# Causal attention and a cosine MLP on one core: score blocks regrouped in PSUM banks, with another order of masks, exponentials and copies

## The chip, the cores and the metric

The kernel runs on one core of a Trainium2 chip. Its time is the device time of one execution in microseconds (us); the lower the better. The kernel before takes 648.55 us, the median of two runs (647.44 and 649.65).

The core has five engines that run their own instruction streams and wait for each other through semaphores: TensorE (PE in the rows; PEld is its weight load), VectorE (DVE), ScalarE (ACT), GpSimd (POOL) and SyncE (SP), which here only starts transfers. TensorE writes its results to PSUM, here one tile `banks` of eight banks with 512 fp32 values per partition, from which VectorE and ScalarE read.

## The reference

4 batches, 12 heads, 448 tokens, head size 64; then 1792 tokens of width 768 through a two-layer MLP of width 2048 with the activation h cos(h), all in fp32.

```python
scores = scale * np.matmul(q, k.transpose(0, 1, 3, 2))
scores = np.where(mask, -1000000000.0, scores)      # causal
scores = scores - np.max(scores, axis=-1, keepdims=True)
attn = np.exp(scores)
attn = attn / (np.sum(attn, axis=-1, keepdims=True) + 1e-09)
attn_out = np.matmul(attn, v)
...
h = x @ w_in
g = h * np.cos(h)
return g @ w_out
```

## The kernel before

**Attention** is a software pipeline over N = 24 pairs of heads (4 batches, 6 pairs each). One turn `i` of the loop in `attention` works on three pairs at once: the scores and softmax of pair `i` (`cur`), the transposition of the probabilities of pair `i - 1` (`prev`), and the product with v of pair `i - 2` (`old`); it also brings q and k of pair `i + 1` (`nxt`) into place. There is no scheduler: each engine does its instructions in the order in which the code writes them, and a pair's blocks are handed over by semaphores.

The 448 tokens are cut into 7 blocks of 64 rows; R is 64, and block `m` (1 to 7) has `m` x 64 columns, since the rest is masked. Both heads of a pair stand in the two halves of the 128 partitions.

- `transpose_in(i, which, b)` (L310) turns q (`which` 0) or k (1) of a pair by four transpositions of 112 tokens into bank `b`; token 4r + c lies at place c of row r in the loaded tile, so that the transposed tokens come out with c outermost. `evac_in` copies the bank on ScalarE to the tile `flat` (L318) and puts them in order by a write with a step of 4 elements (16 bytes). q goes through bank 2, k through bank 7.
- `scores(i)` (L352) computes the 7 blocks in 8 parts (block 7 in two), 16 matmuls of a 64x64 quarter of the array, in the order 7, 5, 7, 4, 6, 3, 2, 1. Blocks whose `SWAP` is 0 (7, 6, 1) and those with 1 (5, 4, 3, 2) use different quarters, so that one of each kind runs at a time: two lanes. `BANK` says where a block lies: 7 and 1 in bank 4, 6 in 5, 5 and 3 in 6, 4 and 2 in 7. `start` and `stop` are set for the first and the last part in a bank.
- `masked` (L361, VectorE) adds the mask, scales, takes the row's minimum, and writes the tile `pb` in SBUF; `exps` (L369, ScalarE) takes the exponential with that minimum as bias and sums it up; `inverse` (L376, L377, VectorE) makes reciprocals of a group of sums; `normalise` (L383, GpSimd) multiplies. The groups are `HIGH` = 7, 6, 5, at the end of a turn, and `LOW` = 4, 3, 2, 1, at the start of the next. The columns of the small tile `stat` go by block number.
- `tp(i, n, b)` (L401) transposes pieces of `pb` in four groups (4, 2, 4 and 4 of them) with `evac_tp` as copy to the tile `pm`: group 0 through bank 3 (copied by VectorE, L316), group 3 through bank 4 (VectorE), group 2 through bank 5 (ScalarE, L318), group 1 through bank 3 again (ScalarE).
- `av` (L427, L437) multiplies with v into banks 0 and 1; `finish_hi` (L453, ScalarE) writes the rounded high part of the result, `finish_lo` (L457, VectorE) the rest, both to `xa` and `xb`, the input of the MLP.
- Between two turns the main loop adds a piece of weight conversion: two VectorE instructions a turn (L139 and L142 in one, L148 and L152 in the next), and one or two on GpSimd (L145; L156, L157), which stand behind the first group of `normalise`.

In the last turns `fill` adds matmuls of the MLP's first layer (L541 to L543). **The MLP** follows (`moe`, L637 and later lines); in it TensorE works through without a pause, and the change does not touch it.

Of the kernel before, what the change touches and what calls it, by code (L numbers as in the profile page):

```python
# [16 lines left out]
ALU = mybir.AluOpType  # L17
# [4 lines left out]
def kernel(  # L22
# [205 lines left out]
    def attention(filler_of, postponed):  # L228
        with (
# [77 lines left out]
            def transpose_in(i, which, b):  # L307
                t = qkt[i, which] = flat[:, 2 * which + i % 2, 0:S], banks8[:, b, 0:S]
                for c in range(4):
                    nc.tensor.transpose(  # L310
                        t[1][:, c * Q4 : (c + 1) * Q4], nat[i][which][:, c], ident[0:Q4, 0:Q4]
                    )
# [45 lines left out]
            def masked(i, *ms):  # L358
                for m in ms:
# [3 lines left out]
                        scalar=3.0e38, op0=ALU.add, op1=ALU.min, accum_out=stats[i][:, 0, m - 1 : m],  # L363
                    )

            def exps(i, *ms):
                for m in ms:
                    st = stats[i]
                    nc.scalar.activation(  # L369
                        probs(i, m), probs(i, m), AF.Exp, scale=-1.0, bias=st[:, 0, m - 1 : m],  # L370
                        accum_out=st[:, 1, m - 1 : m],
                    )

            def inverse(i, ms):
                st, cs = stats[i], slice(min(ms) - 1, max(ms))
# [3 lines left out]
            def normalise(i, *ms):  # L379
                for m in ms:  # L380
                    p = probs(i, m)
                    r = stats[i][:, 2, m - 1 : m]
# [86 lines left out]
            evac_in(0, 1, True, slice(0, 2))  # L469
            evac_in(0, 1, False, slice(2, 4))  # L470
            transpose_in(0, 0, QB)
            evac_in(0, 0, True, slice(0, 2))
            evac_in(0, 0, False, slice(2, 4))
            keep_warm(7)
            for i in range(N + 4):
# [25 lines left out]
                if cur:  # L501
# [879 lines left out]
```

## Time and profile before

| | |
|---|---|
| median of the runs | 648.55 us (647.44 and 649.65) |
| profiled execution, its own time | 651.7 us |
| its span in the profile | 649.7 us |
| busy: TensorE, VectorE, ScalarE, GpSimd | 611.2, 478.2, 426.4, 454.2 us |
| mean granted clock of TensorE | 0.991 of full speed |

The profile shows one execution; times count from the span's start. A row of the timeline is one instruction, or several alike merged, with its start, its length, engine, line, and in brackets how long the engine was idle ahead of it and whom it waited for. `x4` means four instructions. A matmul's length holds its way through the array, so that rows overlap. The MLP's lines cost the most time in sum; the attention loop stands in the first third of the span.

### The profile page before, as it was taken

What the parts mean: (1) busy time and instruction counts of PE and PEld (TensorE: products, weight loads), DVE (VectorE), ACT (ScalarE), POOL (GpSimd) and SP (SyncE); (2) the same over time, 40 slices, a digit from 0 to 9 for tenths busy, and PEclk for the clock granted to TensorE, in tenths of its full rate; (3) what the DMA queues carried; (4) which work ended last, traced back from release to release, by engine and by line L of the source; (5) the groups of instructions that cost most, each with busy time, mean ns of one, the idle gap of its engine ahead of it and who ended that gap; (6) DMA issues with size and microseconds to landing.
All of it is one profiled execution on the core that took longest, in us unless ns stands there. A gap on an engine that the chain in (4) does not pass through costs nothing.

```text
span 649.7 us, 13426 instructions
## 1 busy us (share of the span) xinstructions
PE 611.2 (94%) x4761; PEld 551.5 (85%) x4761; DVE 478.2 (74%) x1016; ACT 426.4 (66%) x929; POOL 454.2 (70%) x529
## 2 busy tenths in 40 slices
PE   6888888888899999999999999999998999999996
PEld 5666666666678999999999999999998999999996
DVE  3588788888773867887777777774347878887886
ACT  3788788888886677877787777752335446544640
POOL 1566666666672597878787877782566888788894
PEclk9799999999999999999999999999998999999999
DMA  7434655544550586879787878859998485558305
GB/s 158 106 93 114 162 126 127 150 116 117 136 162 9 175 301 253 295 283 307 250 294 259 281 278 258 300 201 355 388 338 299 157 292 201 183 201 291 98 2 145
DMA packets 127234, 134.17 MB, mean 207 GB/s; under 512 B 75296, under 2 KB 111504, under 8 KB 127168
## 3 DMA queue, kind: packets, MB, share of 16 engines
q1 hardware_dynamic: 119424, 106.92, 52.8%
q0 software_dynamic: 4928, 24.78, 10.4%
q10 hardware_dynamic: 2816, 1.64, 0.9%
q8 instruction: 37, 0.61, 0.4%
q14 instruction: 29, 0.24, 0.1%
HBM read 83.36 MB, written 49.94 MB: 205 GB/s over the span
## 4 chain that ended last, share of the span: by engine, by line
PE 86%; DVE 6%; ACT 4%; DMA 2%; issue 1%; ACTq 0%; DVEq 0%
PE banks L637 21%; PE banks L1086 11%; PE banks L1066 11%; PE banks L352 7%; PE banks L542 7%; PE banks L541 7%; PE banks L543 7%; PE banks L437 5%; PE banks L310 3%; ACT flat L318 2%; DVE pm L316 2%; PE banks L1103 2%; PE banks L990 2%; PE banks L401 2%; DVE pb L361 2%; ACT pb L369 1%
## 5 line engine op out<-in xcount | busy, mean ns | idle before, releaser
L383 POOL TENSOR_TENSOR pb<-pb,stat 128x448 f32<-128x448 f32 (+6 forms) x168 | 100.5, 627 | 75.0 <-DVE stat L377 68.5
L625 DVE TENSOR_TENSOR acc<-acc,banks 128x768 f32<-128x768 f32 (+1 forms) x122 | 112.7, 932 | 42.8 <-PE banks L637 32.6
L637 PE MATMUL banks<-w,gh 128*128 128x384 f32 x512 | 109.9, 336 | 0.0
L369 ACT ACTIVATE pb<-pb,stat 128x448 f32<-128x448 f32 (+6 forms) x168 | 85.1, 510 | 34.5 <-DVE stat L361 21.7
L637 PEld LDWEIGHTS banks<-w,gh 128*128 128x128 f32 x512 | 90.8, 188 | 1.6 <-DVE acc L623 0.2
L361 DVE CUSTOM_DVE_ANT_0 pb<-banks,mask 128x448 f32<-128x448 f32 (+6 forms) x168 | 60.9, 417 | 30.4 <-PE banks L352 30.4
L541 PE MATMUL banks<-xa,w 128*128 128x512 f32 x192 | 74.9, 390 | 0.4 <-DVE stat L361 0.4
L542 PE MATMUL banks<-xa,w 128*128 128x512 f32 x192 | 75.3, 392 | 0.0
L543 PE MATMUL banks<-xa,w 128*128 128x512 f32 x192 | 75.1, 391 | 0.0
L401 PE MATMUL banks<-ident,pb 128*128 128x128 f32 x336 | 50.6, 281 | 16.0 <-DVE pm L316 15.9
L637 PE MATMUL banks<-w,gl 128*128 128x384 f32 x256 | 65.2, 335 | 0.0
L661 POOL TENSOR_TENSOR w<-ct,w 128x768 fp32r<-128x768 f32 x28 | 51.9, 1852 | 14.7 <-ACT w L660 12.3
L401 PEld LDWEIGHTS banks<-ident,pb 128*128 128x128 f32 x336 | 38.2, 143 | 21.8 <-DVE pm L316 21.2
L352 PE MATMUL banks<-flat 64*64 64x64 f32 (+5 forms) x768 | 49.5, 380 | 7.1 <-DVE pm L316 2.8
L549 ACT ACTIVATE ni<-banks 128x512 int32<-128x512 f32 (+1 forms) x64 | 34.4, 538 | 32.3 <-PE banks L543 18.6
L352 PEld LDWEIGHTS banks<-flat 64*64 64x64 f32 x768 | 33.6, 141 | 25.2 <-ACT flat L318 10.9
L568 POOL TENSOR_TENSOR gl<-r,gh 128x512 fp32r<-128x512 f32 x32 | 41.5, 1299 | 19.3 <-ACT gh L567 19.1
L551 DVE SCALAR_TENSOR_TENSOR r<-ni,banks 128x512 f32<-128x512 int32 (+1 forms) x56 | 35.1, 626 | 21.7 <-ACT ni L549 21.1
L318 ACT COPY flat<-banks 128x448 f32<-128x448 f32 (+1 forms) x48 | 45.8, 953 | 4.0 <-DVE flat L316 4.0
L553 ACT ACTIVATE r<-r 128x512 f32<-128x512 f32 (+1 forms) x56 | 32.8, 586 | 22.5 <-DVE r L551 22.0
L637 PEld LDWEIGHTS banks<-w,gl 128*128 128x128 f32 x256 | 46.4, 188 | 0.0
L1066 PE MATMUL banks<-xb,bb 128*128 128x384 f32 x234 | 45.4, 338 | 0.0
(138 smaller groups left out, 1511.6 us busy)
## 6 DMA issues: line engine op xcount, KB each, us to landing
bb<-w_in_d SPq DMA_DIRECT2D x48, 384.0 KB, 5.2
land<-in_moe_w_in_dram SPq DMA_DIRECT2D x14, 768.0 KB, 5.5
land<-in_moe_w_out_dram SPq DMA_DIRECT2D x14, 768.0 KB, 5.7
w_out_d<-w POOLq DMA_DIRECT2D x14, 768.0 KB, 5.8
big<-w_out_d SPq DMA_DIRECT2D x25, 384.0 KB, 4.7
land<-in_q_dram SPq DMA_DIRECT2D x48, 112.0 KB, 3.3
w_in_d<-w POOLq DMA_DIRECT2D x7, 768.0 KB, 3.9
raw_d<-ct POOLq DMA_DIRECT2D x14, 384.0 KB, 7.8
```

What stands on the lines that cost most here:

```text
L352: nc.tensor.matmul(place(m)[heads(j ^ SWAP[m]), c : c + z - a], lhsT=qt[heads(j), (m - 1) * R : m * R], rhs=kt[heads(j), a:z], start=banks ...
L361: nc.vector.tensor_tensor_reduce(out=probs(i, m), in0=place(m), in1=mask[:, z : z + m * R], scale=-scale, scalar=3.0e38, op0=ALU.add, op1= ...
L369: nc.scalar.activation(probs(i, m), probs(i, m), AF.Exp, scale=-1.0, bias=st[:, 0, m - 1 : m], accum_out=st[:, 1, m - 1 : m],)
L383: nc.gpsimd.tensor_tensor(p, p, r.to_broadcast(list(p.shape)), op=ALU.mult)
L401: nc.tensor.transpose(banks8[:, b, o + x * P : o + (x + 1) * P], prob[i][:, a * R : (a + 2) * R], ident,)
L541: yield nc.tensor.matmul(hv, lhsT=wh[:, f], rhs=x[:, 0, cc, t], start=(cc == 0), stop=False)
L542: yield nc.tensor.matmul(hv, lhsT=wh[:, f], rhs=x[:, 1, cc, t], start=False, stop=False)
L543: yield nc.tensor.matmul(hv, lhsT=wl[:, f], rhs=x[:, 0, cc, t], start=False, stop=(cc == NCC - 1))
L625: nc.vector.tensor_tensor(d, d, o, op=ALU.subtract)
L637: nc.tensor.matmul(o[:, e, 0:EH], lhsT=a[:, cs], rhs=w[:, e * EH : (e + 1) * EH], start=(x == 0), stop=(x == 5),)
L1066: nc.tensor.matmul(o, lhsT=w[:, u, k * P : (k + 1) * P], rhs=x[k][:, v], start=k + m == 0, stop=k == K - 1 and m == 2,)
L1086: nc.tensor.matmul(o[:, b % 2, 0:EH], lhsT=g_ops[i][u][:, c * P : (c + 1) * P], rhs=wouts[g, i][:, v], start=(x == 0), stop=(x == 2),)
```

## The change

- `BANK`, `parts`: block 7 is alone in bank 4; 6 and 1 share bank 5, 5 and 2 bank 6, 4 and 3 bank 7. The parts come in the order 7, 4, 7, 3, 5, 6, 2, 1.
- Masks come in the order 7, 4, 3, 6, 1, 5, 2 (7, 6, 1, 5, 4, 2, 3 before), exponentials in the order 7, 4, 3, 6, 1, 5, 2 (7, 6, 5, 4, 1, 3, 2 before). The groups for reciprocals and normalisation are `FIRST` = 7, 4, 3 and `SECOND` = 6, 1, 5, 2, and the columns of `stat` go by that order. The reciprocals of `FIRST` follow the masks at once; `finish_hi` stands behind four exponentials (behind two before), and `finish_lo` directly behind it in the code.
- k is transposed through bank 6; group 3 of the probabilities goes through bank 5, group 2 through bank 2.
- q's copy reads the bank with a step and writes straight on; k's four transpositions write the bank with a step of 4 elements, and its copy has no step on either side. The two copies of the first pair, which VectorE and ScalarE share, are cut by rows.

The numbers of instructions stay as they are on every engine.

```diff
             def transpose_in(i, which, b):
                 t = qkt[i, which] = flat[:, 2 * which + i % 2, 0:S], banks8[:, b, 0:S]
+                o = t[1].rearrange("p (r c) -> p c r" if which else "p (c r) -> p c r", c=4)
                 for c in range(4):
-                    nc.tensor.transpose(
-                        t[1][:, c * Q4 : (c + 1) * Q4], nat[i][which][:, c], ident[0:Q4, 0:Q4]
-                    )
+                    nc.tensor.transpose(o[:, c], nat[i][which][:, c], ident[0:Q4, 0:Q4])
...
-            def evac_in(i, which, dve=False, cs=slice(0, 4)):
+            def evac_in(i, which, dve=False, rs=slice(0, Q4)):
                 d, s = qkt[i, which]
-                evac(
-                    d.rearrange("p (r c) -> p c r", c=4)[:, cs],
-                    s.rearrange("p (c r) -> p c r", c=4)[:, cs], dve,
-                )
+                d = d.rearrange("p (r c) -> p r c", c=4)
+                s = s.rearrange("p (r c) -> p r c" if which else "p (c r) -> p r c", c=4)
+                evac(d[:, rs], s[:, rs], dve)
...
-            BANK = {7: (4, 0), 1: (4, 7), 6: (5, 0), 5: (6, 0), 3: (6, 5), 4: (7, 0), 2: (7, 4)}
+            BANK = {7: (4, 0), 6: (5, 0), 1: (5, 6), 5: (6, 0), 2: (6, 5), 4: (7, 0), 3: (7, 4)}
             SWAP = {7: 0, 6: 0, 5: 1, 4: 1, 3: 1, 2: 1, 1: 0}
-            HIGH, LOW = (7, 6, 5), (4, 3, 2, 1)
+            FIRST, SECOND = (7, 4, 3), (6, 1, 5, 2)
+            COL = {m: x for x, m in enumerate(FIRST + SECOND)}
...
                 parts = [
-                    (7, 0, 6 * R, 7 * R), (5, 0, 0, 5 * R), (7, R, 0, 6 * R), (4, 0, 0, 4 * R),
-                    (6, 0, 0, 6 * R), (3, 0, 0, 3 * R), (2, 0, 0, 2 * R), (1, 0, 0, R),
+                    (7, 0, 6 * R, 7 * R), (4, 0, 0, 4 * R), (7, R, 0, 6 * R), (3, 0, 0, 3 * R),
+                    (5, 0, 0, 5 * R), (6, 0, 0, 6 * R), (2, 0, 0, 2 * R), (1, 0, 0, R),
                 ]
...
                 if prev:
-                    inverse(i - 1, LOW)
-                    normalise(i - 1, *LOW)
+                    inverse(i - 1, SECOND)
+                    normalise(i - 1, *SECOND)
                 while postponed:
                     postponed.pop(0)()
                 if cur:
                     exps(i, 7)
+                    masked(i, 4, 3)
+                    exps(i, 4, 3)
                     masked(i, 6, 1)
                     exps(i, 6)
-                    masked(i, 5, 4, 2, 3)
+                    masked(i, 5, 2)
+                    inverse(i, FIRST)
+                    normalise(i, *FIRST)
...
                     av(i - 2)
                     finish_hi(i - 2)
-                if cur:
-                    exps(i, 5)
-                    inverse(i, HIGH)
-                    normalise(i, *HIGH)
-                if old:
                     finish_lo(i - 2)
...
                 if cur:
-                    exps(i, 4)
+                    exps(i, 1)
                 if nxt:
-                    transpose_in(i + 1, 1, 7)
+                    transpose_in(i + 1, 1, 6)
                     evac_in(i + 1, 1)
                 if cur:
-                    exps(i, 1, 3)
+                    exps(i, 5)
                 if prev:
-                    tp(i - 1, 3, 4)
-                    evac_tp(i - 1, 3, 4, True)
-                    tp(i - 1, 2, 5)
-                    evac_tp(i - 1, 2, 5)
+                    tp(i - 1, 3, 5)
+                    evac_tp(i - 1, 3, 5, True)
+                    tp(i - 1, 2, QB)
+                    evac_tp(i - 1, 2, QB)
```

In the instruction streams three places show it. First TensorE, at the end of a turn and the start of the next, before: the last two transpositions (`pb`), then the scores (`flat`), with the engines that an instruction waits for in brackets.

```order
L401 MATMUL banks<-ident,pb_143 128x128 [waits DVE_49]
L401 MATMUL banks<-ident,pb_143 128x128
L352 MATMUL banks<-flat 64x64 [waits DVE_49,Activation_49]
L352 MATMUL banks<-flat 64x64
L352 MATMUL banks<-flat 64x320 x2
L352 MATMUL banks<-flat 64x384 x2
L352 MATMUL banks<-flat 64x256 x2
L352 MATMUL banks<-flat 64x384 [waits Activation_49]
L352 MATMUL banks<-flat 64x384
L352 MATMUL banks<-flat 64x192 x2
L352 MATMUL banks<-flat 64x128 x2
L352 MATMUL banks<-flat 64x64 x2
```

The same place now.

```order
L403 MATMUL banks<-ident,pb_143 128x128 [waits DVE_49]
L403 MATMUL banks<-ident,pb_143 128x128
L354 MATMUL banks<-flat 64x64 [waits Activation_49]
L354 MATMUL banks<-flat 64x64
L354 MATMUL banks<-flat 64x256 x2
L354 MATMUL banks<-flat 64x384 x2
L354 MATMUL banks<-flat 64x192 x2
L354 MATMUL banks<-flat 64x320 x2
L354 MATMUL banks<-flat 64x384 [waits DVE_49]
L354 MATMUL banks<-flat 64x384
L354 MATMUL banks<-flat 64x128 x2
L354 MATMUL banks<-flat 64x64 x2
```

The wait for VectorE (its copy of group 3) has moved from the first score to block 6, the sixth part; block 6 no longer waits for ScalarE.

Second VectorE, from the first mask of a turn on, before: masks are the rows `pb,stat<-banks,mask`, and the reading of the row's minimum behind each of them is left out here.

```order
L361 ISA pb_142,stat<-banks,mask 128x448 [waits PE_49]
L376 TENSOR_SCALAR stat<-stat 128x4 [waits Activation_49]
L377 RECIPROCAL stat<-stat 128x4 [waits DVE_49]
L361 ISA pb_142,stat<-banks,mask 128x384
L361 ISA pb_142,stat<-banks,mask 128x64
L361 ISA pb_142,stat<-banks,mask 128x320
L361 ISA pb_142,stat<-banks,mask 128x256
L361 ISA pb_142,stat<-banks,mask 128x128
L361 ISA pb_142,stat<-banks,mask 128x192
L376 TENSOR_SCALAR stat<-stat 128x3 [waits Activation_49]
L377 RECIPROCAL stat<-stat 128x3 [waits DVE_49]
L457 TENSOR_TENSOR xa<-banks,xa 128x128 [waits PE_49]
```

The same place now.

```order
L363 ISA pb_142,stat<-banks,mask 128x448 [waits PE_49]
L378 TENSOR_SCALAR stat<-stat 128x4 [waits Activation_49]
L379 RECIPROCAL stat<-stat 128x4 [waits DVE_49]
L363 ISA pb_142,stat<-banks,mask 128x256 [waits PE_49]
L363 ISA pb_142,stat<-banks,mask 128x192
L363 ISA pb_142,stat<-banks,mask 128x384 [waits PE_49]
L363 ISA pb_142,stat<-banks,mask 128x64
L363 ISA pb_142,stat<-banks,mask 128x320
L363 ISA pb_142,stat<-banks,mask 128x128
L378 TENSOR_SCALAR stat<-stat 128x3 [waits Activation_49]
L379 RECIPROCAL stat<-stat 128x3 [waits DVE_49]
L459 TENSOR_TENSOR xa<-banks,xa 128x128 [waits Activation_49]
```

One wait of the masks for TensorE has become three, at block 7, at block 4 and at block 6; the output's low part, the last row, now has a wait for ScalarE of its own.

Third ScalarE, from the output's high part (the cast) on, before: `flat` are the copies of q and k, `pm` those of the probabilities.

```order
L369 ACTIVATE pb_142,stat<-pb_142,stat 128x384 [waits DVE_49]
L453 CAST xb<-banks 128x448 [waits PE_49]
L369 ACTIVATE pb_142,stat<-pb_142,stat 128x320 [waits DVE_49]
L318 COPY flat<-banks 128x4x112 [waits PE_49,Activation_49]
L369 ACTIVATE pb_142,stat<-pb_142,stat 128x256 [waits DVE_49]
L318 COPY flat<-banks 128x4x112 [waits DVE_49,PE_49,Activation_49]
L369 ACTIVATE pb_142,stat<-pb_142,stat 128x64
L369 ACTIVATE pb_142,stat<-pb_142,stat 128x192 [waits DVE_49]
```

The same place now, with the exponentials that come before it in the turn.

```order
L371 ACTIVATE pb_142,stat<-pb_142,stat 128x256 [waits DVE_49]
L371 ACTIVATE pb_142,stat<-pb_142,stat 128x192 [waits DVE_49]
L371 ACTIVATE pb_142,stat<-pb_142,stat 128x384 [waits DVE_49]
L455 CAST xb<-banks 128x448 [waits PE_49]
L317 COPY flat<-banks 128x448 [waits PE_49,Activation_49]
L371 ACTIVATE pb_142,stat<-pb_142,stat 128x64 [waits DVE_49]
L317 COPY flat<-banks 128x448 [waits DVE_49,PE_49,Activation_49]
L371 ACTIVATE pb_142,stat<-pb_142,stat 128x320
```

The exponentials of blocks 4 and 3 have moved ahead of the cast, that of block 5 behind both copies.

## Rows read from the trace of the kernel before

**Rows 1.** Busy time by stretch: us, each engine (instructions), TensorE's clock, DMA share, GB/s.
```profile
33.47:183.92 150.45, 129.90 (x1960) 101.55 (x1961) 122.61 (x467) 126.00 (x388) 99.91 (x171) 1.00 0.53 131
213.18:481.00 267.82, 267.82 (x1384) 247.28 (x1384) 193.56 (x242) 186.33 (x287) 197.31 (x184) 1.00 0.81 283
...
18.00:20.00 2.00, 2.00 (x22) 1.45 (x18) 0.00 (x0) 0.23 (x2) 0.08 (x1) 0.51 0.76 148
```
**Rows 2.** Chain of work that ended last: start us, us, what.
```profile
33.47 1.94 PE banks L352 x22
...
183.92 1.93 PE banks L352 x22
```
**Rows 3.** Waits of VectorE, 56 to 184 us: in total, times, longest.
```profile
DVE pb L361 <- PE banks L352: 14.7, 17, 1.0
```
**Rows 4.** Timeline of TensorE, 100.5 to 116 us; the weight load from a narrower view.
```profile
100.76 1.86 PE L352 MATMUL banks<-flat 64*64 64x64 f32 x29 [0.25 <-ACT pb L369]
...
101.71 0.55 PEld L352 LDWEIGHTS banks<-flat 64*64 64x64 f32 x14 [0.21 <-ACT pm L318]
...
105.72 1.04 PE L401 MATMUL banks<-ident,pb 128*128 128x128 f32 x8
107.40 0.44 PE L401 MATMUL banks<-ident,pb 128*128 128x128 f32 x2 [0.65 <-DVE pm L316]
108.09 1.94 PE L352 MATMUL banks<-flat 64*64 64x64 f32 x29 [0.25 <-DVE pm L316]
```
**Rows 5.** Timeline of VectorE, 100.5 to 116 us; the last row from 197.5 to 198.6.
```profile
102.73 0.62 DVE L361 CUSTOM_DVE_ANT_0 pb<-banks,mask 128x448 f32<-128x448 f32 x1 [0.81 <-PE banks L352]
...
105.86 0.17 DVE L376 TENSOR_SCALAR stat<-stat 128x3 f32<-128x3 f32 x1 [0.36 <-ACT pb L369]
...
106.16 0.59 DVE L457 TENSOR_TENSOR xa<-banks,xa 128x448 fp32r<-128x448 f32 x1
106.67 1.28 DVE L316 COPY pm<-banks 128x512 f32<-128x512 f32 x2
107.86 0.61 DVE L139 TENSOR_SCALAR ct<-st 128x256 uint32<-128x256 uint32 x1
108.50 0.83 DVE L142 SCALAR_TENSOR_TENSOR ct<-st,ct 128x256 uint32<-128x256 uint32 x1
110.25 0.62 DVE L361 CUSTOM_DVE_ANT_0 pb<-banks,mask 128x448 f32<-128x448 f32 x1 [0.92 <-PE banks L352]
...
197.80 0.28 DVE L139 TENSOR_SCALAR ct<-st 128x256 uint32<-128x256 uint32 x1
```
**Rows 6.** Timeline of ScalarE, 100.5 to 116 us.
```profile
103.46 0.67 ACT L369 ACTIVATE pb<-pb,stat 128x448 f32<-128x448 f32 x1 [1.15 <-DVE stat L376]
...
104.15 0.62 ACT L369 ACTIVATE pb<-pb,stat 128x384 f32<-128x384 f32 x1
...
104.76 0.51 ACT L453 CAST xa<-banks 128x448 fp32r<-128x448 f32 x1
...
105.73 0.98 ACT L318 COPY flat<-banks 128x448 f32<-128x448 f32 x1
106.49 0.50 ACT L369 ACTIVATE pb<-pb,stat 128x256 f32<-128x256 f32 x1
...
106.97 0.97 ACT L318 COPY flat<-banks 128x448 f32<-128x448 f32 x1
...
108.05 0.46 ACT L369 ACTIVATE pb<-pb,stat 128x192 f32<-128x192 f32 x1
```
**Rows 7.** Groups by line and form, 56 to 115 us: busy us, mean ns.
```profile
L318 ACT COPY flat<-banks 128x448 f32<-128x448 f32 x16 | 15.5, 969 | 0.0
...
L453 ACT CAST xa<-banks 128x448 fp32r<-128x448 f32 x8 | 4.1, 511 | 0.0
```
**Rows 8.** Timeline of GpSimd, 100.5 to 116 us.
```profile
103.81 1.69 POOL L383 TENSOR_TENSOR pb<-pb,stat 128x256 f32<-128x256 f32 x4 [2.15 <-DVE stat L377]
...
106.60 2.45 POOL L383 TENSOR_TENSOR pb<-pb,stat 128x448 f32<-128x448 f32 x3
```

More of the change, by code (lines that the diff above doesn't have):

```diff
@@ L318, in evac, with col @@
                     nc.scalar.copy(dst, src)
-            def evac_in(i, which, dve=False, cs=slice(0, 4)):
+            def evac_in(i, which, dve=False, rs=slice(0, Q4)):
                 d, s = qkt[i, which]
-                evac(
-                    d.rearrange("p (r c) -> p c r", c=4)[:, cs],
-                    s.rearrange("p (c r) -> p c r", c=4)[:, cs], dve,
-                )
+                d = d.rearrange("p (r c) -> p r c", c=4)
+                s = s.rearrange("p (r c) -> p r c" if which else "p (c r) -> p r c", c=4)
+                evac(d[:, rs], s[:, rs], dve)
             AT = {5: 0, 1: 5, 3: 6, 7: 9, 6: 16, 4: 22, 2: 26}
-            BANK = {7: (4, 0), 1: (4, 7), 6: (5, 0), 5: (6, 0), 3: (6, 5), 4: (7, 0), 2: (7, 4)}
+            BANK = {7: (4, 0), 6: (5, 0), 1: (5, 6), 5: (6, 0), 2: (6, 5), 4: (7, 0), 3: (7, 4)}
             SWAP = {7: 0, 6: 0, 5: 1, 4: 1, 3: 1, 2: 1, 1: 0}
-            HIGH, LOW = (7, 6, 5), (4, 3, 2, 1)
+            FIRST, SECOND = (7, 4, 3), (6, 1, 5, 2)
+            COL = {m: x for x, m in enumerate(FIRST + SECOND)}
+            def col(m):
+                return slice(COL[m], COL[m] + 1)
             def open_step(i):
@@ L362, in masked @@
                         out=probs(i, m), in0=place(m), in1=mask[:, z : z + m * R], scale=-scale,
-                        scalar=3.0e38, op0=ALU.add, op1=ALU.min, accum_out=stats[i][:, 0, m - 1 : m],
+                        scalar=3.0e38, op0=ALU.add, op1=ALU.min, accum_out=stats[i][:, 0, col(m)],
                     )
@@ L369, in exps @@
                     nc.scalar.activation(
-                        probs(i, m), probs(i, m), AF.Exp, scale=-1.0, bias=st[:, 0, m - 1 : m],
-                        accum_out=st[:, 1, m - 1 : m],
+                        probs(i, m), probs(i, m), AF.Exp, scale=-1.0, bias=st[:, 0, col(m)],
+                        accum_out=st[:, 1, col(m)],
                     )
             def inverse(i, ms):
-                st, cs = stats[i], slice(min(ms) - 1, max(ms))
+                st, cs = stats[i], slice(COL[ms[0]], COL[ms[-1]] + 1)
                 nc.vector.tensor_scalar(st[:, 2, cs], st[:, 1, cs], 1e-9, None, op0=ALU.add)
@@ L381, in normalise @@
                     p = probs(i, m)
-                    r = stats[i][:, 2, m - 1 : m]
+                    r = stats[i][:, 2, col(m)]
                     nc.gpsimd.tensor_tensor(p, p, r.to_broadcast(list(p.shape)), op=ALU.mult)
@@ L468, in attention @@
             transpose_in(0, 1, 7)
-            evac_in(0, 1, True, slice(0, 2))
-            evac_in(0, 1, False, slice(2, 4))
+            evac_in(0, 1, True, slice(0, Q4 // 2))
+            evac_in(0, 1, False, slice(Q4 // 2, Q4))
             transpose_in(0, 0, QB)
-            evac_in(0, 0, True, slice(0, 2))
-            evac_in(0, 0, False, slice(2, 4))
+            evac_in(0, 0, True, slice(0, Q4 // 2))
+            evac_in(0, 0, False, slice(Q4 // 2, Q4))
             keep_warm(7)
```

## The prediction

> **What bounds the kernel now.** I read the busy time in two stretches first [rows 1]. From 213 to 481 us TensorE is busy without a gap (267.82 of 267.82 us); nothing that attention does changes the length of that part, it only sets where it begins. In the attention loop, from 33.47 to 183.92 us, no engine is full: TensorE is busy 129.90, ScalarE 126.00, VectorE 122.61 and GpSimd 99.91 of 150.45 us. The chain that ended last dates the steps by their scores (L352), 20 steps between the two rows shown [rows 2]: 7.52 us each. An engine's own work would allow 6.5 us (129.90 / 20), so a step is a circle of waits.
>
> Of the waits in 17 steps, VectorE's mask for the scores is the one to look at: 17 times, 14.7 us, 0.86 each [rows 3]. One step in time, from 100.76: the scores start at 100.76 and the first mask only at 102.73 [rows 4, 5], 1.97 us later (2.16 in the next step, 108.09 to 110.25), though it is the mask of block 7, the third of eight parts that TensorE writes. It waits until all scores (to 102.62) are through, since block 1, the last part, lies in the same bank 4. Inside the scores a weight load also stands 0.21 us for ScalarE's copy out of bank 5 [rows 4]. Then VectorE masks until 105.50, waits 0.36 for the exponential of block 5, and runs the reciprocals, the output's low part (L457), two copies and the weight conversion, up to 109.33 [rows 5]. The next scores start at 108.09, right behind those two copies (to 107.95), because their first target, bank 4, is only free with the second copy: 7.33 us.
>
> **The change, part by part.** I count from M, the start of the first mask.
>
> *Banks by time.* Block 7 is alone in bank 4 and ends with the third part: in its lane of TensorE (blocks 7, 6, 1, together 896 columns) 448 columns are done, half. Half of the scores' 1.86 us plus the 0.11 from last score to mask (102.62 to 102.73) gives 1.04 us from scores to mask in place of 1.97. Masks 4 and 3 need the fourth part, the others the last; VectorE comes to its second mask at least 0.62 us behind the first (the first one's length [rows 5]), when they are there. Two waits leave the scores. Their first matmul no longer waits for the second copy (the transpositions that fed it go to bank 5, which block 6 needs as the sixth part), and block 6 no longer waits for ScalarE's copy (that one moves to bank 2), 0.21 us. The scores can follow the last two transpositions directly: eight took 1.04 us [rows 4], so two 0.26 to 0.28, and 107.40 + 0.28 is 0.41 us earlier than 108.09.
>
> *Order of exponentials.* Ahead of the output's high part (L453) now stand four (7, 4, 3, 6) instead of two. The first starts at M+0.73 (103.46); with their durations 0.67, 0.50, 0.46, 0.62 and the cast's 0.51 [rows 6] the high part is there at M+3.49. VectorE is through with the masks at M+2.77 (105.50) and with the reciprocals 0.30 later (105.86 to 106.16), at M+3.07: its 0.36 wait for an exponential goes, since the third is done at M+2.36 or so, but it now waits for the cast, 0.44 us with the hand-over. The low part starts at M+3.51, today at M+3.43: nothing is gained there, the stall only moves by one instruction. Behind it on VectorE stand both copies, the weight conversion and the next masks.
>
> *The new circle.* VectorE: masks 2.77, reciprocals 0.30, wait 0.44, low part 0.51, copies 1.19 (106.67 to 107.86), weights 1.47 (to 109.33) [rows 5]: 6.68 us, and then the next M, if the scores are there. They are: the first copy ends at M+4.62, TensorE's last transpositions start 0.13 later (now 107.27, half of the two copies, to 107.40), the scores 0.28 later at M+5.03, and block 7 is ready at M+6.07, 0.6 us early. ScalarE: its turn with the cast ends at M+3.49, then come q's copy (0.76 until the next starts), k's copy and the exponential of 1 (1.08 together, 106.97 to 108.05) [rows 6]: k is ready by M+5.33 or a little later, block 7 at M+6.4. q's copy also holds bank 2, where the third group of transpositions now goes: from M+3.4 to M+4.4, that group to M+4.95, the scores at M+5.25, block 7 at M+6.3. So VectorE becomes the bound: **6.7 us**, 0.85 less than 7.52 with rounding.
>
> *Copies and transpositions of q and k.* Both copies write today with a step of 16 bytes and take 0.97 us; a cast of as many elements without steps takes 0.51 [rows 7]. k's copy has no step any more: 0.51. q's copy reads with steps instead, which no row shows: between 0.51 and, if reading costs twice the stepped write, 1.94 us; I take 0.97, the nearest row. Through bank 2 it starts to cost beyond 1.3 us (4.95 + 0.3 + 1.04 leaves 0.4 to 6.68). k's four transpositions now write with a step of 16 bytes, which no row shows either: 0.52 us for four if nothing changes (half of the eight's 1.04), 0.99 if they stretch as the stepped copy does (0.97 to 0.51); I take 0.52. TensorE has the time: they start when mask 2 frees bank 6 at about M+2.8, the eight follow, to M+4.4, and then TensorE waits until M+4.75 for the first copy, 0.35 us, with 0.6 more to spare ahead of the mask. So 0.95 us more cost nothing.
>
> The Trainium skill (PSUM — Partial Sum Buffer, Specifications) says that PSUM has lines of 8 bytes and that any access pattern that isn't contiguous slows matmuls significantly, which would be k's transposition here. No run so far shows such a write of TensorE, and the page gives no factor; by the slack above the sum stays as it is up to 2.8 times the price.
>
> *GpSimd.* Its two groups of normalisations become equal, 14 and 14 blocks of 64 columns where now 10 take 1.69 and 18 take 2.45 us [rows 8]: about 2.1 each. The one at a step's start begins at M+1.08 (103.81) as now and ends at M+3.2, block 6 first in it and ready ahead of TensorE's first transpositions, block 2 last and ready as TensorE comes to it (M+3.7). With the weights between (105.50 to 106.60) GpSimd works 5.2 us of 6.7. VectorE's conversions are dearer beside it (L139 takes 0.61 there, 0.28 where GpSimd rests [rows 5]); they will stand beside it as now, and I keep their price, with 0.3 us a step as a possible gain.
>
> *DMA.* No transfer is added, and the engines' share in the loop is 0.53 [rows 1]: hidden.
>
> **Sum.** 20 steps x 0.85 = 17.0 us. The early steps run at half clock in part (0.51 from 18 to 20 us [rows 1]) and wait for their loads: three of them, between 0 and 2.6, I take 1.5. The last step, from 183.92, is cut by the first matmuls of the next part: between 0 and 1.3, I take 0.9. Together 19.4 us of the profiled execution's 651.7 (649.7 span and 2.0 around it): 632.3. The median of the runs lies 3.15 us lower, at 648.55; from there it is 629.15, and I predict **629 us**.
>
> **Rivals.**
> *The early bank brings nothing*: the mask still sees its scores only when all are through. Then 1.97 - 0.21 = 1.76 from scores to mask, a step of 5.03 + 1.76 = 6.79, or 6.98 with the other step's 2.16: 0.54 to 0.73 gained, 11 to 15 us, 634 to 638. For it: VectorE waited for TensorE in each of 17 steps. Against: block 7's bank is closed by the third part, as the order shows.
> *The wait only moves.* If one of the four exponentials comes 0.8 us late (masks 4 and 3 delayed by their scores, or the cast behind them), the low part, both copies and the next scores do so too, and a step stays at 7.4 to 7.5: 645 to 649. For it: the low part starts no earlier against M than now, and nothing on VectorE itself becomes shorter. Against: by the sum masks and scores are there 0.1 to 0.6 us before they are needed.
> *q's read is dear.* At 1.94 us, 0.97 more, bank 2 holds up the transpositions and block 7 comes at M+7.25: 0.27 gained a step, 5 in all, 643.
> *The other side: k's stepped transposition.* It eats the gain when the four cost 0.95 + 0.85 = 1.8 us more, 2.3 us or 4.5 times as much; beyond that the kernel is slower. At eight times (3.6 more) a step is 9.35 us and 23 of them cost 42 us more than now: 690. For it speaks only that a stepped copy on another engine takes 1.9 times as long; against, that 4.5 is far from that. The Trainium skill's rule in the page named above puts the trouble exactly there.
>
> **How the numbers follow.** Forecast 0.61, early bank without effect 0.14, wait only moves 0.13, q dear 0.05, slower 0.07. The likeliest one's own range is 620 to 634: below, VectorE's conversions free of GpSimd (20 x 0.3 = 6 us) and all of the early and last steps (1.5 to 3); above, steps of 6.95. For 8 in 10 I go from 619 to 641, which takes in the first rival. A measurement of this kernel can tell about 2% from no change, 13 us: faster by more are the forecast and the better part of the first rival, 0.71; within 2% the rest of it, q and the moved wait, 0.22; slower 0.07.
>
> **What would show it.** Steps of 6.5 to 6.8 us between the first scores; the first mask 1.0 to 1.7 us behind the scores' start, with no wait of VectorE for TensorE; in its place a wait of 0.4 to 0.5 us of the low part (L459) for ScalarE's cast; no weight load of the scores that waits for ScalarE's pm copy; k's copy at 0.5 to 0.6 us; k's four transpositions under 1.0. It would be wrong if those took over 1.5 us, if a wait for GpSimd stood ahead of the later transpositions, or if VectorE still waited for scores.

## The result, and the profile of the changed kernel

The changed kernel takes 616.37 us, the median of two runs (616.31 and 616.42): 32.2 us less than before, a ratio of 0.950 (95% interval 0.943 to 0.957). The profiled execution took 616.31 us with a span of 614.3, against 651.7 and 649.7. I had predicted 629 with a range of 619 to 641. The direction and the mechanism were right; the gain is two thirds larger than forecast and lies below the range.

The spans differ by 35.35 us. Cut at the starts of the scores, and at the first matmul of `moe`:

| stretch | before, us | after, us | difference | predicted |
|---|---|---|---|---|
| start to the first scores | 9.21 | 7.81 | -1.40 | none |
| steps 0 to 2 | 24.26 | 17.94 | -6.32 | -1.5 |
| 20 steps | 150.45 | 125.38 | -25.07 | -17.0 |
| last step, up to `moe` | 29.10 | 28.33 | -0.77 | -0.9 |
| `moe` | 436.65 | 434.87 | -1.78 | none |

The change doesn't touch the MLP. In the profiled execution of before TensorE ran 3.4 us of it at the lower clock, half of full speed, which by estimate costs 1.7 us; after has no such stretch there, and of the kernels below some have one and some not (the MLP takes 434.2 to 439.9 us in the ten profiles). That stretch of before, by windows (start and end, length, each engine's busy time with its instructions, granted clock, DMA share, GB/s).

```profile
491.10:494.40 3.30, 3.30 (x12) 3.30 (x12) 2.98 (x6) 2.40 (x6) 1.38 (x2) 0.50 0.93 345
```

Then the attention loop of after, in the same columns; it answers to the first row of [rows 1].

```profile
25.75:151.13 125.38, 121.99 (x1961) 101.62 (x1960) 115.37 (x467) 111.93 (x388) 100.09 (x169) 1.00 0.63 155
```

The same instructions (1961, 467, 388) now fill their engines: TensorE 97% of the time, where it was 86%, VectorE 92% where it was 81%. A step takes 6.27 us on average, mostly 6.17 to 6.21; 6.47 from 100 to 126 us, where a pair's output lies across `xa` and `xb` and both its parts take two instructions.

One step of after: TensorE's scores and the transpositions of q and k, against [rows 4].

```profile
87.66 1.74 PE L354 MATMUL banks<-flat 64*64 64x64 f32 x32
...
91.04 0.60 PE L311 MATMUL banks<-ident,land 112*128 112x112 f32 x4
...
91.92 0.55 PE L311 MATMUL banks<-ident,land 112*128 112x112 f32 x4
...
93.86 1.74 PE L354 MATMUL banks<-flat 64*64 64x64 f32 x32
```

VectorE in that step, against [rows 5]: the first mask, the output's low part, both copies, the conversion, the next mask.

```profile
88.79 0.62 DVE L363 CUSTOM_DVE_ANT_0 pb<-banks,mask 128x448 f32<-128x448 f32 x1
...
92.22 0.62 DVE L459 TENSOR_TENSOR xa<-banks,xa 128x448 fp32r<-128x448 f32 x1 [0.31 <-ACT xa L455]
...
92.76 1.28 DVE L315 COPY pm<-banks 128x512 f32<-128x512 f32 x2
...
93.95 0.41 DVE L148 SCALAR_TENSOR_TENSOR ct<-st,ct 128x256 uint32<-128x256 uint32 x1
...
94.47 0.54 DVE L152 SCALAR_TENSOR_TENSOR ct<-st,ct 128x256 f32<-128x256 f32 x1
...
94.94 0.61 DVE L363 CUSTOM_DVE_ANT_0 pb<-banks,mask 128x448 f32<-128x448 f32 x1
```

The reader is to see three things. The mask follows the scores' start by 1.13 and 1.08 us with no wait in brackets (1.97 and 2.16 before). The scores are one run from 93.86, with no weight load waiting for ScalarE, and start 5.07 us behind the mask. VectorE waits once, 0.31 us, for ScalarE's cast. The two costliest waits of VectorE from 56 to 160 us (total, times, longest), against [rows 3]:

```profile
DVE xa L459 <- ACT xa L455: 2.1, 6, 0.4
DVE xa L459 <- ACT xb L455: 2.0, 5, 0.4
```

VectorE's third and last wait in this view is of the same kind, 1.4 us; the wait for scores is gone from it. What closes the circle now is told by the chain of waits over one step (start, us, what):

```profile
83.27 2.29 ACT pb L371 x8
85.56 0.43 ACT xa L455
...
86.01 0.62 DVE xa L459
86.63 1.20 DVE pm L315 x2
87.83 0.21 DVE ct L139
...
88.07 0.64 DVE ct L142
...
88.79 0.62 DVE pb L363
```

Four exponentials and the cast on ScalarE, then VectorE from the low part to the next mask: 6.19 us from one such turn to the next (83.27 to 89.46). TensorE is not in it.

### The profile page after: what moved, and what is told of

It reads as the page before. It is cut to its first block, busy times and chain, and to the rows that moved or that the text cites. A ratio compares the mean times of both kernels' runs of the same rounds, so it can differ in the third digit from the quotient of the medians.

```text
span 614.3 us, 13427 instructions
## 1 busy us (share of the span) xinstructions
PE 597.9 (97%) x4761; PEld 547.2 (89%) x4761; DVE 470.4 (77%) x1016; ACT 409.4 (67%) x929; POOL 455.4 (74%) x529
## 4 chain that ended last, share of the span: by engine, by line
PE 80%; DVE 9%; ACT 8%; DMA 2%; issue 1%; ACTq 0%; DVEq 0%
PE banks L638 22%; PE banks L1087 12%; PE banks L1067 12%; PE banks L543 7%; PE banks L544 7%; PE banks L542 7%; ACT pb L371 6%; DVE pm L315 3%; PE banks L354 3%; PE banks L439 2%; PE banks L1104 2%; PE banks L991 2%; PE banks L403 2%; DVE xa L459 2%; DVE pb L363 1%; DMA bb<-w_in_d 1%
## 5 line engine op out<-in xcount | busy, mean ns | idle before, releaser
L385 POOL TENSOR_TENSOR pb<-pb,stat 128x448 f32<-128x448 f32 (+6 forms) x168 | 102.3, 639 | 40.0 <-DVE stat L379 37.7
L557 DVE SCALAR_TENSOR_TENSOR r<-r,banks 128x512 f32<-128x512 f32 (+1 forms) x56 | 35.0, 626 | 13.6 <-ACT r L555 13.6
L354 PE MATMUL banks<-flat 64*64 64x64 f32 (+5 forms) x768 | 44.3, 371 | 0.6 <-ACT flat L317 0.6
L354 PEld LDWEIGHTS banks<-flat 64*64 64x64 f32 x768 | 32.1, 138 | 13.3 <-issue 3.9
```

The lines of the kernel that those rows point to most:

```text
L354: nc.tensor.matmul(place(m)[heads(j ^ SWAP[m]), c : c + z - a], lhsT=qt[heads(j), (m - 1) * R : m * R], rhs=kt[heads(j), a:z], start=banks ...
L385: nc.gpsimd.tensor_tensor(p, p, r.to_broadcast(list(p.shape)), op=ALU.mult)
```

## The experiments

The theory, called A: the banks take away VectorE's wait for the scores, the step is then VectorE's own work plus the wait for the cast, and the two things that I had put at nothing, the order and the copies, matter where they touch that circle. Rivals were that the copies or the order bring most of it by themselves. I undid each part of the change in the changed kernel (the `u_` kernels), did each alone in the kernel before (`d_`), and then changed what stands in the new circle. All are timed against the kernel before on the same chip, which took 648.47 us beside the first four and 649.61 beside the last four.

### One block moved back to its old bank (u_bank1)

```diff
-            BANK = {7: (4, 0), 6: (5, 0), 1: (5, 6), 5: (6, 0), 2: (6, 5), 4: (7, 0), 3: (7, 4)}
+            BANK = {7: (4, 0), 1: (4, 7), 6: (5, 0), 5: (6, 0), 2: (6, 5), 4: (7, 0), 3: (7, 4)}
```

> The changed kernel with one thing undone: block 1 lies in bank 4 again, with block 7 (nothing else moves; bank 5 holds block 6 alone). Theory A (a step is VectorE's own work, and the early bank is what lets VectorE start its mask right behind its conversion): the first mask waits for all scores again, 1.85 us from scores to mask where 1.08 are seen now, so a step is 5.07 + 1.85 = 6.9 us instead of 6.2 and the kernel takes about 14 to 18 us more, 630 to 634. Theory B (the step was carried by ScalarE's chain, and the cheap copies of q and k made the gain): 616 to 620, the mask's wait is made up elsewhere.

Measured: 640.42 us, ratio 0.987 (0.983 to 0.991), 24 us above the changed kernel. The costliest of VectorE's waits from 56 to 160 us (total, times, longest, here and in the kernels that follow):

```profile
DVE pb L363 <- PE banks L354: 9.6, 15, 0.8
```

and one of these waits in the timeline:

```profile
94.61 0.62 DVE L363 CUSTOM_DVE_ANT_0 pb<-banks,mask 128x448 f32<-128x448 f32 x1 [0.68 <-PE banks L354]
```

The wait is back, the mask comes 1.83 and 1.93 us behind the scores by turns, and a step takes 7.00 us. A block of 64 columns that shares a bank with block 7 holds block 7's mask until the last part is written: the mechanism of theory A. Its price is larger than I gave it (630 to 634): the spans of the profiled executions lie 22.6 us apart, of which 0.73 us in each of 20 steps make 14.6, steps 0 to 2 make 3.5, the start and the last step 1.6; 2.9 lie in the MLP, for which I have no cause.

### The transpositions and copies undone (u_copies)

```diff
-                o = t[1].rearrange("p (r c) -> p c r" if which else "p (c r) -> p c r", c=4)
                 for c in range(4):
-                    nc.tensor.transpose(o[:, c], nat[i][which][:, c], ident[0:Q4, 0:Q4])
+                    nc.tensor.transpose(
+                        t[1][:, c * Q4 : (c + 1) * Q4], nat[i][which][:, c], ident[0:Q4, 0:Q4]
+                    )
...
-                d = d.rearrange("p (r c) -> p r c", c=4)
-                s = s.rearrange("p (r c) -> p r c" if which else "p (c r) -> p r c", c=4)
-                evac(d[:, rs], s[:, rs], dve)
+                evac(
+                    d.rearrange("p (r c) -> p c r", c=4)[:, cs],
+                    s.rearrange("p (c r) -> p c r", c=4)[:, cs], dve,
+                )
...
```

(and the copies of the first pair cut by columns again.)

> The changed kernel with the transpositions and copies of q and k as before (both copies write with a step of 16 bytes, about 0.97 us each instead of 0.53). Theory A: ScalarE rests 0.60 us a step in the changed kernel, and the old copies put 0.67 us on it, so a step grows by 0.1 to 0.2 us: 618 to 622 us. Theory B (cheap copies made the gain): a step grows by the full 0.67 or more, 630 us and above.

Measured: 625.06 us, ratio 0.963 (0.960 to 0.966), 8.7 above the changed kernel; a step takes 6.54. What TensorE and VectorE wait for from 56 to 160 us:

```profile
PE banks L356 <- ACT flat L318: 3.4, 16, 0.2
PE banks L405 <- ACT flat L318: 2.9, 13, 0.3
DVE pb L365 <- PE banks L356: 2.8, 10, 0.4
```

Copies of 0.98 us (the mean of 18) make the transpositions and the scores wait, then the mask. In a step of 7.5 us the long copies were nearly covered; in one of 6.2 they are not. The time lies between the two theories' numbers.

### The order undone (u_order)

```diff
-            FIRST, SECOND = (7, 4, 3), (6, 1, 5, 2)
+            HIGH, LOW = (7, 6, 5), (4, 3, 2, 1)
...
-                    masked(i, 4, 3)
-                    exps(i, 4, 3)
                     masked(i, 6, 1)
                     exps(i, 6)
-                    masked(i, 5, 2)
-                    inverse(i, FIRST)
-                    normalise(i, *FIRST)
+                    masked(i, 5, 4, 2, 3)
...
                     finish_hi(i - 2)
+                if cur:
+                    exps(i, 5)
+                    inverse(i, HIGH)
+                    normalise(i, *HIGH)
...
```

(with the reciprocals and multiplications of the other group, the later exponentials and the columns of `stat` to match.)

> The changed kernel with the order of masks, exponentials and sums as before (groups 7, 6, 5 and 4, 3, 2, 1; the high part behind two exponentials), with the new banks and the new copies. Theory A: the group of 7, 6 and 5 (18 blocks of 64 columns) stands beside VectorE's conversions again, which then take 1.3 to 1.45 us a step instead of 1.0, and VectorE waits 0.36 for an exponential again: a step of 6.5, 6 us more in all, 621 to 624. Theory C (the order is worth nothing, the conversions got shorter for another reason): 615 to 618, conversions at 1.0 us.

Measured: 629.26 us, ratio 0.970 (0.966 to 0.973), 12.9 above the changed kernel and more than theory A gave it (621 to 624); a step takes 6.74. VectorE's reciprocals wait for the exponential of block 5 as before the change, and the conversions are long again. The wait, from 56 to 160 us:

```profile
DVE stat L374 <- ACT pb L367: 7.2, 16, 0.5
```

and three of VectorE's groups by form, from 50 to 110 us (busy us, mean ns, idle before):

```profile
L142 DVE SCALAR_TENSOR_TENSOR ct<-st,ct 128x256 uint32<-128x256 uint32 x5 | 4.1, 826 | 0.2
L374 DVE TENSOR_SCALAR stat<-stat 128x3 f32<-128x3 f32 x9 | 3.7, 416 | 4.1 <-ACT pb L367 4.1
L152 DVE SCALAR_TENSOR_TENSOR ct<-st,ct 128x256 f32<-128x256 f32 x4 | 3.0, 755 | 0.4
```

The wait, 0.45 us each, is about as long as the one for the cast that takes its place in the changed kernel. What the order brings is in the length of VectorE's work. One part is L374: 0.17 us alone, it took 0.72 in every second step, where GpSimd's L157 had begun just ahead of it; theory A did not have this. The other part is the two conversions, which in the changed kernel take, in the same view:

```profile
L142 DVE SCALAR_TENSOR_TENSOR ct<-st,ct 128x256 uint32<-128x256 uint32 x5 | 3.5, 697 | 0.2
L152 DVE SCALAR_TENSOR_TENSOR ct<-st,ct 128x256 f32<-128x256 f32 x5 | 2.6, 519 | 0.5
```

GpSimd's second group of multiplications tells why. In the timeline of the kernel with the old order it is

```profile
92.90 2.44 POOL L381 TENSOR_TENSOR pb<-pb,stat 128x448 f32<-128x448 f32 x3 [0.41 <-DVE stat L375]
```

and in that of the changed kernel

```profile
92.54 2.19 POOL L385 TENSOR_TENSOR pb<-pb,stat 128x448 f32<-128x448 f32 x3
```

The steps alternate: one has L139 and L142, the next L148 and L152. The old group ends at 95.34, and L142 beside it (94.80 to 95.62) 0.28 us later; the new one ends at 94.73, and L152 beside it (94.47 to 95.01) again 0.28 later. From 30 to 150 us, in all profiles with this group, a conversion that begins beside one of its multiplications either takes its free length (0.28 us L139, 0.42 the others) or, where that multiplication ends too late for it, ends 0.28 us behind that end (L139 0.15). So what counts is not when the group is done but when the one multiplication beside the conversion is. In the kernel before, blocks 6 and 5 hold both conversions of a step: these two multiplications, taken one by one from narrower windows,

```profile
107.49 0.83 POOL L383 TENSOR_TENSOR pb<-pb,stat 128x384 f32<-128x384 f32 x1
...
108.28 0.77 POOL L383 TENSOR_TENSOR pb<-pb,stat 128x320 f32<-128x320 f32 x1
```

end at 108.32 and 109.05, L139 and L142 at 108.47 and 109.33 [rows 5]. With the new order the first conversion mostly begins 0.05 to 0.09 us ahead of the end of the multiplication beside it and takes its free length, and one is held: L142 (88.07 to 88.80) by block 4,

```profile
87.75 0.76 POOL L385 TENSOR_TENSOR pb<-pb,stat 128x256 f32<-128x256 f32 x1
```

or L152 by block 3, which is the end of the row of 92.54. From the start of the first to the end of the second it is 1.05 and 1.06 us in these two steps, and 1.27 to 1.41 with the old order.

### The banks alone (d_banks)

```diff
-            BANK = {7: (4, 0), 1: (4, 7), 6: (5, 0), 5: (6, 0), 3: (6, 5), 4: (7, 0), 2: (7, 4)}
+            BANK = {7: (4, 0), 6: (5, 0), 1: (5, 6), 5: (6, 0), 2: (6, 5), 4: (7, 0), 3: (7, 4)}
...
-                    transpose_in(i + 1, 1, 7)
+                    transpose_in(i + 1, 1, 6)
...
-                    tp(i - 1, 3, 4)
-                    evac_tp(i - 1, 3, 4, True)
-                    tp(i - 1, 2, 5)
-                    evac_tp(i - 1, 2, 5)
+                    tp(i - 1, 3, 5)
+                    evac_tp(i - 1, 3, 5, True)
+                    tp(i - 1, 2, QB)
+                    evac_tp(i - 1, 2, QB)
```

(with the new order of the parts.)

> The kernel before with the banks alone: the new places of the blocks, the new order of the score parts, the new banks of the transpositions; masks, exponentials, groups and copies as before. Theory A: most of the gain, a step of 6.5 to 6.7 us with conversions at 1.4 us beside GpSimd: 622 to 628. Theory B: little of it, 640 or more.

Measured: 633.62 us, ratio 0.976 (0.972 to 0.981), 14.9 below before; a step takes 6.82. The wait for scores is gone, and two others have come up in its place:

```profile
DVE stat L376 <- ACT pb L369: 8.1, 15, 0.7
...
PE banks L401 <- ACT flat L318: 5.2, 16, 0.5
```

The first is what the order was to end, the second is the copy out of bank 2. This is the likeliest cause that the banks alone fall short of theory A's 622 to 628; no run takes the two away one by one.

### The copies alone, and the order alone (d_copies, d_order)

Both are the reverse of the diffs above, made in the kernel before.

> The kernel before with the new transposition and copies of q and k alone. Theory A (a step of before is the circle scores, masks, two exponentials, low part, VectorE's two copies, scores; ScalarE's copies lie beside it): both copies at 0.53 us and no use of it, steps of 7.4 to 7.5, 644 to 648 us. Theory D (the parts add up: the changed kernel is 9 us faster than the one with the old copies, so the copies alone bring 9 us here too): 638 to 641.

> The kernel before with the new order of masks, exponentials, sums and groups alone; banks and copies as before. Theory A: VectorE's conversions get shorter, to about 1.0 us, and its wait for the scores grows by as much; the low part starts no earlier against the first mask (3.43 us behind it in both profiles); steps of 7.3 to 7.5, 642 to 648 us. Theory D (the parts add up: the order is worth 13 us in the changed kernel): 634 to 637.

Measured: the copies alone give 643.75 us, ratio 0.991 (0.988 to 0.994), 5.9 below before, with a step of 7.33; the order alone gives 649.32, ratio 1.000 (0.997 to 1.002). Both lie just outside theory A's ranges (644 to 648 and 642 to 648), but nearer to them than to those of parts that add up (638 to 641 and 634 to 637). VectorE's wait for the scores, from 56 to 160 us, with the copies alone:

```profile
DVE pb L359 <- PE banks L350: 10.4, 15, 0.8
```

and with the order alone:

```profile
DVE pb L365 <- PE banks L356: 15.3, 14, 1.3
```

Before it was 0.86 us a time [rows 3]; with the order alone it is 1.09, though the conversions are about as short as in the changed kernel (L142 0.72, L152 0.54 us): VectorE is done earlier and only waits longer for scores that come no earlier. The rival that the order or the copies bring most of it falls.

### One group of GpSimd left out (a_nonorm)

```diff
                     inverse(i, FIRST)
-                    normalise(i, *FIRST)
```

> The changed kernel without the normalisation of blocks 7, 4 and 3 (GpSimd's group at the end of a step is left out, so the output is not attention). Theory A (VectorE's conversions are longer when GpSimd works beside them): L139 0.28, L142 0.43, L148 and L152 0.42 us as where GpSimd rests, 0.2 to 0.3 us a step less on VectorE; but a step gains less than 0.1 of it, because the scores of block 7 are only there 5.07 + 1.08 = 6.15 us behind the mask before: 613 to 616 us, and VectorE waits 0.1 to 0.25 us a step for scores. Rival (GpSimd has nothing to do with it): the conversions stay at 0.37, 0.67, 0.50 and 0.51.

Measured: 615.63 us, ratio 0.948 (0.943 to 0.953); a step takes 6.19. The same two groups of VectorE, in the same view:

```profile
L142 DVE SCALAR_TENSOR_TENSOR ct<-st,ct 128x256 uint32<-128x256 uint32 x5 | 2.1, 425 | 0.2
L152 DVE SCALAR_TENSOR_TENSOR ct<-st,ct 128x256 f32<-128x256 f32 x5 | 2.1, 425 | 0.5
```

and a wait of VectorE that has come back, from 56 to 160 us:

```profile
DVE pb L363 <- PE banks L354: 1.5, 8, 0.2
```

Nothing on VectorE was edited, and L142 went from 697 to 425 ns, L152 from 519 to 425: it is GpSimd's work beside them that stretches them. The step wins little by it, since the mask then waits for the scores again: two circles of nearly the same length stand side by side at about 6.15.

### The cast ahead of an exponential (cast_early)

```diff
                     masked(i, 6, 1)
-                    exps(i, 6)
                     masked(i, 5, 2)
...
                     finish_lo(i - 2)
+                if cur:
+                    exps(i, 6)
```

> The changed kernel with the exponential of block 6 moved behind the output's high part, so that only three exponentials stand ahead of it. Theory A (the wait of VectorE's low part for the high part, 0.31 to 0.38 us a step, is on both circles): that wait goes, the first copy and the scores come about 0.3 us earlier, until TensorE's own work of about 6.0 us a step is the bound: 20 x 0.2 = 4 us less, 611 to 614. Rival (TensorE is the bound already): 615 to 618.

Measured: 615.49 us, ratio 0.948 (0.943 to 0.953); a step takes 6.08. The stretch from 30 to 90 us in the changed kernel:

```profile
30.00:90.00 60.00, 58.62 (x954) 49.13 (x954) 55.17 (x218) 53.89 (x183) 49.47 (x83) 1.00 0.62 148
```

and in this one:

```profile
30.00:90.00 60.00, 59.81 (x977) 50.32 (x977) 58.61 (x227) 55.12 (x188) 49.94 (x84) 1.00 0.63 149
```

The end of one step in its chain of waits:

```profile
88.81 1.48 PE banks L439 x28
90.29 0.53 PE banks L311 x4
...
91.67 1.27 PE banks L403 x10
92.94 1.67 PE banks L354 x23
```

All of it is TensorE's; in every second step 0.42 us of q's copy stand in the chain as well. VectorE's wait for the cast is gone, and TensorE works through (59.81 of 60 us). But VectorE is nearly full too (58.61): its conversions begin 0.45 us earlier behind the mask, so that GpSimd holds both of them again, and take 1.37 to 1.45 us. By the busy times neither engine leaves much more of a step to gain. The loop gains 0.19 us a step, some 3.8 us in 20, as theory A had it; but the profiled execution gives more than that back outside the loop: 3.4 us in the MLP (1.7 by a stretch at half clock, as in before), 1.2 in the last step, 1.1 ahead of the first scores, against 0.5 gained in steps 0 to 2. The median lies in the rival's range (615 to 618). The medians, 615.49 and 616.37, were taken beside different runs of before, and don't tell the two kernels apart.

## Why the prediction was right and where it was wrong

Forecast were 19.4 us of the span, measured 35.35. Of the 16.0 us between them 8.1 lie in the 20 steps, 4.8 in the early steps, 1.8 in the MLP and 1.4 ahead of the first scores.

**The bank of block 7: right.** Forecast were 1.04 us from scores to mask, measured 1.08 to 1.14; moving block 1 back alone costs 24 us. The rival that the early bank brings nothing (1.76 us) is out.

**The scores' two waits: right.** They follow the first copy, 5.07 us behind the mask (forecast 5.03), and wait for no copy out of bank 5.

**The new wait: right.** The low part waits 0.31 to 0.38 us for the cast (forecast 0.44), and starts 3.43 behind the mask (forecast 3.51). The rival that the wait only moves is out at the 0.8 us that it needed.

**VectorE's conversions: the term that was mis-sized in the loop.** The circle's terms, forecast and then measured from 88.79 to 94.94: up to the low part 3.51 and 3.43, low part 0.51 and 0.54, copies 1.19 and 1.19, conversion 1.47 and 0.99 (1.04 in the other kind of step). So 6.68 became 6.15 to 6.2, and 0.43 to 0.48 of the difference is this one term. I had seen that L139 takes 0.28 us where GpSimd rests and 0.61 beside it, kept the price, and set 0.3 a step aside as a possible gain. The step that failed is "they will stand beside it as now": I had worked out how long GpSimd's second group is (2.1 us where it was 2.45), and not which of its multiplications each conversion would meet. Now block 4 or 3 stands where block 6 or 5 did, and mostly one conversion a step is held where it was two. `u_order` (old groups, both held again) and `a_nonorm` (no group, none held) show it. The Trainium skill (SBUF — State Buffer, Who interferes with whom) says that VectorE and GpSimd share a pair of SBUF ports and that a VectorE instruction with two inputs in SBUF contends with GpSimd's reads. The trace agrees: L142 and L152, which read two tiles, are held until 0.28 us behind the end of the multiplication beside them, and the masks, which read PSUM beside SBUF, are not (0.62 us in every kernel). L139, which reads one tile, and L374 are held as well, so that two inputs are not the only case here.

**The early steps: mis-sized.** I gave three of them 1.5 us, at most 2.6, which is 0.85 each, the price at full clock; they gave 6.32. The first masks of the first and the third step, before:

```profile
12.55 0.62 DVE L361 CUSTOM_DVE_ANT_0 pb<-banks,mask 128x448 f32<-128x448 f32 x1 [4.08 <-PE banks L352]
...
28.11 0.62 DVE L361 CUSTOM_DVE_ANT_0 pb<-banks,mask 128x448 f32<-128x448 f32 x1 [2.98 <-PE banks L352]
```

and after:

```profile
9.62 0.62 DVE L363 CUSTOM_DVE_ANT_0 pb<-banks,mask 128x448 f32<-128x448 f32 x1 [2.37 <-PE banks L354]
...
20.68 0.62 DVE L363 CUSTOM_DVE_ANT_0 pb<-banks,mask 128x448 f32<-128x448 f32 x1 [0.99 <-PE banks L354]
```

The scores of these steps started at 9.21 and 25.61 before, so they took 3.34 and 2.50 us to the mask (3.15 in the step between); after, from 7.81 and 19.54, it is 1.81 and 1.14 (1.16). That is 4.9 of the 6.3 us. A wait for matmuls costs more where they run at half clock, so its removal also brings more. Before's second and third scores lie in stretches at half clock, by windows:

```profile
16.60:20.00 3.40, 2.77 (x26) 2.12 (x30) 0.00 (x0) 1.62 (x7) 1.48 (x3) 0.51 0.72 150
...
23.40:26.80 3.40, 3.40 (x26) 2.90 (x28) 1.35 (x3) 3.40 (x12) 2.40 (x3) 0.50 0.49 111
```

In after the first scores lie in one (7.70 to 11.10 us, 0.50), and the second run into another when block 7 is nearly done (its mask is at 14.96):

```profile
14.50:17.90 3.40, 3.40 (x30) 2.64 (x23) 2.89 (x17) 2.46 (x11) 2.27 (x5) 0.50 0.68 161
```

What the banks alone bring at half clock, `d_banks` shows: its second scores, from 16.57, lie in such a stretch too (0.51 from 15.80 to 19.30) and take 1.81 us to the mask where before's took 3.15. That is 1.34 us, where the loop at full clock gained 0.90 to 1.02. The first step gained 1.53; before's windows show no lower clock there, but its first scores are as long in the chain as its second, 3.25 and 3.12 us (1.94 in the loop). What is left of the second and third step goes by this reckoning to the clock itself. The low clock stood in [rows 1], and I didn't multiply by it. Ahead of both falls in before TensorE had been busy 0.85 of 3.50 and 1.75 of 3.40 us. Of the other kernels those with the old banks (`d_copies`, `d_order`) show two such falls between 15 and 27 us, those with new ones one or none. That the shorter waits spare the second fall fits this, but no run isolates it, and it stays open.

**The first scores, 1.40 us earlier: mostly not the change.** In the chain up to them the halves of the first copy take 0.40 (VectorE) and 0.35 us (ScalarE) where before had 0.57 and 0.56: these 0.38 us are the change's, and `u_bank1`, `a_nonorm` and `cast_early` have the same lengths. k's load took 4.23 us in place of 4.52; in the profiles below it varies from 3.98 to 4.95. The other 0.7 us are TensorE's: four transpositions 0.59 in place of 0.99, and seven matmuls of L285 0.58 in place of 0.90. They are short in this one profile alone: its eight first transpositions take 0.96 us, those of the nine others 1.73. The windows show a clock of 1.00 there in both kernels, and no row tells why.

**The copies: hidden as forecast in price, not in cover.** q's copy, which reads with a step, took 0.52 us, as k's without one; I had taken 0.97. All of them in after, against [rows 7]:

```profile
L317 ACT COPY flat<-banks 128x448 f32<-128x448 f32 x19 | 9.9, 522 | 0.0
```

The sum had named no gain for them: in a step of 6.68 us it found 0.4 to 0.6 us to spare ahead of the mask. Undoing them costs 8.7 us: at 6.2 us a step that room is gone, and they count.

**k's stepped write: right, and the other side is out.** Its four transpositions take 0.55 us, q's without a step 0.60, both 0.60 before; in `u_copies`, where k's write has no step either, they take 0.55 and 0.60 as well. The Trainium skill's rule (PSUM — Partial Sum Buffer, Specifications), by which an access pattern that isn't contiguous slows matmuls significantly, is not borne out by this trace for a 4-byte write with a step of 16 bytes.

**TensorE's own work was read too high.** I wrote that it allowed 6.5 us a step, 129.90 over 20. The same 1961 matmuls are busy 121.99 us after, and `cast_early` runs steps of 6.08: the busy time of before held matmuls stretched while they waited. The scores are a part of it, with a weight load that waited inside (1.86 to 1.94 us a step busy, 1.74 after: 2.4 to 4 of the 7.9 us); the rest is not traced. This did not enter the sum, but as a floor it would have forbidden the result.

**The parts don't add up.** Alone they bring 14.9 (banks), 5.9 (copies) and 0.3 us (order), 21 in all; together 32.2. Taken away from the changed kernel, the order costs 12.9 and the copies 8.7. While the mask waits for scores, shorter work on VectorE only makes it wait longer (`d_order`); once the banks have ended that wait, the same edit shortens the step. I had put the order and the copies at nothing: in the old circle they are worth little, in one of 6.68 us there was room for them, and the step of 6.2 us that came has none.

## What to carry to other kernels

In this kernel blocks that share a PSUM bank become readable together (`u_bank1`: 0.64 us of waiting in each step, 24 us in all), so pair them by when they are written and used, not by what fills the bank. When a change opens a new circle, cost every other part of it again in that circle, also those that came out at nothing in the old one, and there ask above all what an engine beside it does to the length of its instructions: which instruction of the other engine each one meets, and when that one ends. Where a stretch runs at half clock, cost a wait for matmuls there apart: here it was worth 1.34 us where it was 0.90 to 1.02 at full clock.

## What the runs showed of the hardware

- A ScalarE copy of 128x448 fp32 out of PSUM takes 0.52 us with a step of 448 bytes in its read, as without a step, and 0.97 with a step of 16 bytes in its write to SBUF.
- Four 112x112 fp32 transpositions that write PSUM with a step of 16 bytes take 0.55 to 0.60 us, the same as contiguous ones.
- VectorE's 128x256 conversions that read two SBUF tiles take 0.42 us with a GpSimd group left out. Beside it they still take 0.41 to 0.43 where the multiplication that they begin beside ends early enough, and otherwise end 0.28 us behind its end, which made them 0.48 to 0.83 us long.
